# A decode attention and feed-forward kernel: products written over the keys, the output weights in two loads at the end, queries spread by two matmuls, quotients turned per 16 heads

## The chip, the cores and the metric

The kernel runs on one core of one Trainium2 chip. The metric is the device time of one execution in microseconds (us). A core has five engines that run side by side: TensorE (PE, matmuls and transposes; in a profile its weight loads stand apart as PEld), VectorE (DVE), ScalarE (ACT), GpSimd (POOL) and SyncE (SP), which here issues every transfer. Sixteen DMA engines move data between the HBM memory and SBUF, the core's working memory of 128 partitions; matmuls write to PSUM.

## The reference

One new token for each of four batch rows, model width 512, 32 heads of 128, 4096 cached keys and values per head, everything float32. The output mixes an attention block and a gated feed-forward block by a gate computed from the input:

```python
q = (x @ wq).reshape(B, Sq, H, Dh).transpose(0, 2, 1, 3)
scores = einsum("bhqd,bhkd->bhqk", q, k_cache) * (Dh ** -0.5)
p = softmax(scores, axis=-1)
o = einsum("bhqk,bhkd->bhqd", p, v_cache)
a = o.transpose(0, 2, 1, 3).reshape(B, Sq, H * Dh) @ wo
b = (gelu(x @ w_gate) * (x @ w_up)) @ w_down
g = sigmoid((x * gate_w).sum(-1, keepdims=True))
out = g * a + (1 - g) * b
```

With B = 4, H = 32, 4096 keys and Dh = 128, each cache has 268 MB. The weights wq and wo have 8.4 MB each, w_gate, w_up and w_down 3.7 MB each.

## The kernel before, in words

**Tiles.** The caches are cut into 64 tiles of keys and 64 of values. Tile i holds two heads (HT = 2) of one batch row: group g = i // 4, row b = i % 4. Each head has 64 partitions, and a partition holds 64 keys (or values) of 128 numbers, 32 KB in one piece. A tile has 4 MiB.

**Buffers and transfers.** A pool `kv` of five buffers of 32 KB a partition (NB = 5) takes every large load: wq in two halves, keys, values, the two feed-forward inputs (behind the values of 19 and 20) and w_down. The list `loads` (L79) fixes their order; `load_next` (L88) allocates a buffer for the next entry and issues its transfer on SP's queue. SP runs in program order, so a load that waits for its buffer holds back all loads behind it. A values load takes the buffer of a key tile, a keys load that of a values tile. wo comes apart from the list, in eight loads of 1 MB into a buffer of its own (`load_wo`, L95), each waiting for the matmuls that used the one before. w_down comes in four pieces, as the last transfer.

**Queries.** `po` holds x @ wq; eight PE transposes and eight copies make `QT` (L160 to L168). `q_spread` (L175) brings the queries of a group to all partitions of their head: eight matmuls of 128 columns, with a column of `QT` as broadcast weights.

**Scores.** There is one query per head and row, so scores are made on VectorE: `products` (L191) multiplies a part of the key tile by the query, `sums` (L203) adds up each 128. A tile is done in four parts (`MOST`, L34): four keys of the 64 whose sums ScalarE takes ("A", L209), and three times 20 with a VectorE sum ("D", L206). Products go to buffers of their own (`pa`, `pr`). The last two tiles give ScalarE more (`LAST`).

**Softmax.** `max_a` (L223) takes the maximum per partition and transposes it on PE; `soft_max` (L229) takes the maximum per head, spreads it by matmuls (L235), and lets ScalarE write the exponentials into `PM` and their sums into `RS` (L240). `pv` (L253) multiplies them by the values in 16 matmuls of 512 columns; a float32 matmul is two records in the trace, so 32 records.

**Output.** After the four rows of a group, `gather` (L265) copies the accumulated values and adds them up by matmuls, `weigh` (L275) divides by the sums of exponentials and turns the quotients by eight small matmuls (L286) into `oT`; after every second group `project_a` (L289) multiplies them by a quarter-megabyte slice of wo per step (L251) into `a_acc`. The feed-forward part runs inside tiles 20 and 21 (`ffn_up`, `ffn_gelu`) and `ffn_down` at the end.

**Order.** The program is written out by hand: each engine runs its instructions in the order in which the loop (L335) emits them. In iteration i VectorE makes the scores of tile i with the softmax of i-1 between its first parts, while PE does the values of i-1 and, behind them, the transpose of the maximum of i. In the last two iterations this order is changed so that maxima come earlier (L345 to L353).

Of the kernel before, what the change touches and what calls it, by code (L numbers as in the profile page):

```python
# [17 lines left out]
def tile_gated_mix(ctx: ExitStack, tc: tile.TileContext, x, kc, vc, wq, wo, w_gate, w_up, w_down, gate_w, out):  # L18
    nc = tc.nc
    P = 128  # L20
# [12 lines left out]

    MOST = (("A", 60, 64), ("D", 0, 20), ("D", 20, 40), ("D", 40, 60))  # L34
    LAST = (("U", 48, 56), ("A", 60, 64), ("D", 0, 20), ("U", 40, 48), ("A", 56, 60), ("D", 20, 40))
    NL = 2
    FFN_AT = 20
    FG = 512
# [9 lines left out]
    dump = head.tile([P, D], F32)  # L48
# [11 lines left out]
    def load(kind, i):  # L60
        t = T[kind, i] = kv.tile([P, TW], F32, name="kv")
        if kind in "kv":
            h, b = HT * (i // B), i % B
            src = (kc if kind == "k" else vc)[b, h:h + HT].rearrange("h (p r) d -> (h p) (r d)", p=PH)
            n = 2 if (kind, i) == ("v", NT - 1) else 1
            for s in range(n):
                nc.sync.dma_start(t[:, s * TW // n:(s + 1) * TW // n], src[:, s * TW // n:(s + 1) * TW // n])  # L67
        elif kind == "q":
            nc.sync.dma_start(t, wq.rearrange("(p c) n -> p (c n)", c=KC)[:, i * TW:(i + 1) * TW])
        elif kind == "f":  # L70
            nc.sync.dma_start(t[:, :KC * F], (w_gate, w_up)[i].rearrange("(p c) n -> p (c n)", c=KC))
        else:
            for f0 in range(0, F, FG):
                f1 = min(f0 + FG, F)
                n = (f1 - f0) // P
                nc.sync.dma_start(t[:, f0 // P * DM:(f0 // P + n) * DM],
                                  w_down[f0:f1].rearrange("(p i) n -> p (i n)", i=n))

    loads = [("q", 0), ("q", 1), ("k", 0)]  # L79
    for i in range(NT):  # L80
# [11 lines left out]

    WO = {}

    def load_wo(w):  # L95
        WO[w] = work.tile([P, 4, DM], F32, name="wo_sb", bufs=1)
        nc.sync.dma_start(WO[w], wo[w * 4 * D:(w + 1) * 4 * D, :].rearrange("(p e) n -> p e n", e=4))
# [52 lines left out]
    q_sb = work.tile([P, HG, D], F32, name="wo_sb", bufs=1)  # L150
    for c in range(KC):
        w = T["q", c // 2].rearrange("p (c n) -> p c n", c=2)[:, c % 2, :]
        for s in range(2):
            for j in range(4):
                n0 = (j * HG + s * HB) * D
                nc.tensor.matmul(PO[s][32 * j:32 * j + 32].rearrange("p j d -> p (j d)"), xT[:, c, :32],
                                 w[:, n0:n0 + HB * D], start=c == 0, stop=c == KC - 1)
    for s in range(2):
        nc.scalar.activation(q_sb[:, s * HB:(s + 1) * HB, :], PO[s], AF.Copy)
    QT = consts.tile([P, 4, HG, B], F32)  # L160
    for s in range(2):
        ps = ps1.tile([P, HB, P], F32, name="q")
        for a in range(HB):
            nc.tensor.transpose(ps[:, a, :], q_sb[:, s * HB + a, :], ident)
        for a in range(HB):
            nc.vector.tensor_copy(QT[:, :, s * HB + a, :],  # L166
                                  ps[:, a, :].rearrange("p (j b k) -> p j b k", j=4, b=B)[:, :, :, 0])
    QT = QT.rearrange("p j a b -> p (j a) b")  # L168
# [17 lines left out]
    u = consts.tile([P, 2, FG], F32)  # L186

    def parts(i):
        return LAST if i >= NT - NL else MOST

    def products(i, o):  # L191
        kind, r0, r1 = o
        g, b = divmod(i, B)
        n = r1 - r0
        if kind == "U":
            t = u.rearrange("p s (r d) -> p (s r) d", d=D)
        else:
            t = work.tile([P, n, D], F32, name="pa" if kind == "A" else "pr", bufs=1)
        nc.vector.tensor_tensor(t, T["k", i].rearrange("p (r d) -> p r d", d=D)[:, r0:r1],  # L199
                                QB[g][:, b:b + 1, :].to_broadcast([P, n, D]), op=OP.mult)  # L200
        return t

    def sums(i, o, t):  # L203
        kind, r0, r1 = o
        if kind == "D":
            nc.vector.tensor_reduce(SC[i][:, r0:r1], t, axis=AX.X, op=OP.add)  # L206
        else:
            for r in range(r0, r1):
                nc.scalar.activation(dump, t[:, r - r0, :], AF.Copy, accum_out=SC[i][:, r:r + 1])  # L209

    def scores_a(i):
        SC[i] = work.tile([P, R], F32, name="sc")
        return products(i, parts(i)[0])

    def scores(i, first):
        sums(i, parts(i)[0], first)
        for o in parts(i)[1:]:
            sums(i, o, products(i, o))
# [10 lines left out]
    def soft_max(i):  # L229
# [3 lines left out]
        nbp = ps2.tile([P, 1], F32, name="sm")  # L233
        for h in range(HT):
            nc.tensor.matmul(nbp[h * PH:(h + 1) * PH, :], ones[:1, :PH], m2[:, h:h + 1], start=True, stop=True)  # L235
        nb = work.tile([P, 1], F32, name="nb")
        nc.scalar.activation(nb, nbp, AF.Copy, scale=-scale)  # L237
        for h in range(HT):
            s = slice(h * PH, (h + 1) * PH)
            nc.scalar.activation(PM[i % 2][:, PZ:].rearrange("p (c m) -> p c m", m=32)[s, :, h:RJ * HT:HT],  # L240
                                 SC[i][s, :].rearrange("p (c j) -> p c j", j=RJ), AF.Exp, bias=nb[s, :], scale=scale,
# [32 lines left out]

    def weigh(g):  # L275
        ri = work.tile([B * HT, 1], F32, name="ri")
        nc.vector.reciprocal(ri, OS[g][:, D:])
        on = work.tile([B * HT, 4, D // 4], F32, name="on")
        nc.vector.tensor_scalar(on, OS[g][:, :D].rearrange("p (k e) -> p e k", e=4), ri, None, op0=OP.mult)  # L279
        w, r = divmod(g, 2)  # L280
        if r == 0:
            OT[w] = ps1.tile([P, 4, 32], F32, name="oT")
        for h in range(HT):
            q = 32 * (HT * r + h)
            for e in range(4):
                nc.tensor.matmul(OT[w][q:q + 32, e, :], on[:, e, :], hsel[:, h].rearrange("p b k -> p (b k)"),  # L286
                                 start=True, stop=True)

    def project_a(w):  # L289
        ot = work.tile([P, 4, 32], F32, name="ot")  # L290
        nc.scalar.activation(ot, OT[w], AF.Copy)
        for e in range(4):
            project(a_acc, ot[:, e, :], WO[w][:, e, :], (w, e) == (0, 0), (w, e) == (H // 4 - 1, 3))


    hT = consts.tile([P, F // P, 32], F32)

    def ffn_up(s):
        ps = ps1.tile([P, FG], F32, name="q")
        rest = F % FG  # L300
        nc.vector.memset(ps[32 * (F // FG):, rest:], 0.0)
        for c in range(KC):
            for j in range(4):
                n = min(FG, F - j * FG)
                nc.tensor.matmul(ps[32 * j:32 * j + 32, :n], xT[:, c, :32],
                                 T["f", s][:, c * F + j * FG:c * F + j * FG + n], start=c == 0, stop=c == KC - 1)
        nc.scalar.activation(u[:, s], ps, AF.Copy)

    def ffn_gelu():
        x1 = u[:, 0]  # L310
        s = T["f", 1].rearrange("p (a n) -> p a n", n=FG)
        t1, t2, t3, th, y, v = (s[:, a, :] for a in range(6))
# [5 lines left out]
        nc.vector.scalar_tensor_tensor(v, y, 0.5, u[:, 1], op0=OP.mult, op1=OP.mult)  # L318
        for j0, j1 in ((0, F // FG), (F // FG, 4)):
            w = min(FG, F - j0 * FG)  # L320
            n = w // P
# [89 lines left out]
```

## Time and profile before

| | before |
|---|---|
| median of 3 runs (lowest, highest) | 1318.66 us (1318.5, 1318.79) |
| the profiled execution, its own time | 1318.34 us |
| its span in the profile | 1316.6 us |
| VectorE busy | 1157.2 us (88%) |
| PE busy, PEld busy | 495.5 us (38%), 176.0 us (13%) |
| ScalarE busy | 210.5 us (16%) |
| moved by the DMA engines | 565.28 MB, 429 GB/s over the span |
| keys load: issue to landing, median | 42.3 us |
| values load: issue to landing, median | 33.5 us |

The span is what the profiler saw between the first and the last instruction; the profiled execution's own time is 1.74 us longer. In a row of a group, "x190 | 535.8, 2820 | 6.5" means 190 instructions, 535.8 us in sum, 2820 ns each on average, and 6.5 us of idle time just before them, with what ended it. In the chain and the timeline the first number is the start and the second the duration, both in us. The row of DMA digits gives the busy share of the 16 engines in tenths, in 40 equal slices. Queue q1 carries the kernel's transfers; q8 and q14 carry the engines' instructions.

### The profile page before, as it was taken

The page shows a single profiled execution, that of the slowest core. Times are in us where ns is not written, and L with a number is a line of the kernel's source. Part 1 is how long each engine was busy: PE and PEld are TensorE (multiplying, and loading weights), DVE is VectorE, ACT ScalarE, POOL GpSimd, SP SyncE. Part 2 cuts the span into 40 slices and gives each one's busy share as a digit, 9 for nine tenths or more (in the row PEclk, how much of TensorE's full clock was granted, in tenths as well). Part 3 has the DMA queues.
Part 4 walks back from the last instruction along what each step waited for, and adds up shares of the span by engine and source line. Part 5 has one row for each costly group of instructions (what it writes and reads, how often), then busy time and mean ns, then how long its engine had stood idle before and what let it go on. Part 6 is the DMA issues. An engine that isn't in the chain of part 4 may idle for free.

```text
span 1316.6 us, 9351 instructions
## 1 busy us (share of the span) xinstructions
PE 495.5 (38%) x3562; PEld 176.0 (13%) x3562; DVE 1157.2 (88%) x645; ACT 210.5 (16%) x963; POOL 0.7 (0%) x6
## 2 busy tenths in 40 slices
PE   3242434342441452433344243342433333343327
PEld 1011112110110110201112011110101111011102
DVE  1999899989999579998999989899899989999894
ACT  0111111101111111101101101101101101111133
POOL 0000000000000000000000000000000000000000
PEclk9566666666666676766666665776766765676667
DMA  9999999999999999999999999999999999999997
GB/s 411 433 429 430 432 433 437 433 430 431 431 436 434 428 435 432 432 433 437 430 432 432 433 438 431 433 432 431 433 434 432 433 433 430 436 434 430 434 430 331
DMA packets 21096, 565.28 MB, mean 429 GB/s; under 512 B 2472, under 2 KB 2488, under 8 KB 2620
## 3 DMA queue, kind: packets, MB, share of 16 engines
q1 hardware_dynamic: 21052, 564.69, 99.5%
q8 instruction: 28, 0.46, 0.1%
q14 instruction: 16, 0.13, 0.0%
HBM read 564.67 MB, written 0.01 MB: 429 GB/s over the span
## 4 chain that ended last, share of the span: by engine, by line
DMA 67%; DVE 29%; PE 2%; issue 1%; another core or an unknown queue 0%; SPq 0%; ACT 0%; DVEq 0%; ACTq 0%
DMA kv<-in_A_k_cache 54%; DVE pr L199 15%; DVE sc L206 12%; DMA kv<-in_A_v_cache 10%; DMA kv<-in_B_w_down 2%; PE po L258 2%; DVE pa L199 1%; DVE m L232 0%; SPq L67 0%; PE b_acc L251 0%; DVE u L199 0%; DVE on L279 0%; PE sm L138 0%; DVE m L225 0%
## 5 line engine op out<-in xcount | busy, mean ns | idle before, releaser
L258 PE MATMUL po<-kv,pm 128*32 128x512 f32 x2048 | 365.1, 877 | 489.0 <-DMA kv<-in_A_v_cache 486.4
L206 DVE TENSOR_REDUCE sc<-pr 128x20 f32<-128x2560 f32 x190 | 535.8, 2820 | 6.5
L199 DVE TENSOR_TENSOR pr<-kv,qb 128x2560 f32<-128x2560 f32 x190 | 535.3, 2817 | 4.2
L258 PEld LDWEIGHTS po<-kv,pm 128*32 128x32 f32 x2048 | 91.1, 154 | 707.4 <-issue 692.1
L199 DVE TENSOR_TENSOR pa<-kv,qb 128x512 f32<-128x512 f32 x66 | 45.5, 690 | 85.8 <-DMA kv<-in_A_k_cache 85.8
L237 ACT ACTIVATE nb<-sm 128x1 f32<-128x1 f32 x64 | 10.9, 170 | 573.4 <-PE sm L235 573.2
L227 PE MATMUL sm<-ident,m 128*1 128x128 f32 x64 | 19.2, 300 | 206.1 <-DVE m L225 205.9
L209 ACT ACTIVATE dump<-pa 128x128 f32<-128x128 f32 x264 | 81.7, 309 | 10.4 <-DVE pa L199 2.6
L235 PE MATMUL sm<-m,ones 1*64 1x1 f32 x256 | 22.3, 238 | 85.9 <-DVE m L232 85.9
L182 ACT ACTIVATE qb<-q 128x512 f32<-128x512 f32 x16 | 9.6, 597 | 258.6 <-PE q L179 258.6
L209 ACT ACTIVATION_READ_ACCUMULATOR dump<-pa 128x1 f32 x264 | 49.2, 186 | 0.0
L240 ACT ACTIVATE pm<-sc,nb 64x64 f32<-64x64 f32 x128 | 44.5, 348 | 3.0 <-ACT nb L237 0.2
L267 ACT ACTIVATE o<-po 128x512 f32<-128x512 f32 x16 | 9.6, 597 | 191.2 <-PE po L258 191.2
L227 PEld LDWEIGHTS sm<-ident,m 128*1 128x1 f32 x64 | 5.1, 79 | 250.7 <-issue 219.3
L235 PEld LDWEIGHTS sm<-m,ones 1*64 1x64 f32 x256 | 17.0, 181 | 103.8 <-DVE m L232 96.3
L179 PE MATMUL q<-ident,QT 128*64 128x128 f32 x256 | 24.9, 357 | 0.6 <-DVE QT L166 0.6
L240 ACT ACTIVATION_READ_ACCUMULATOR pm<-sc,nb 64x1 f32 x128 | 23.6, 185 | 0.0
L270 PE MATMUL sm<-o,sel 128*8 128x128 f32 x128 | 16.6, 273 | 10.7 <-ACT o L267 10.7
L179 PEld LDWEIGHTS q<-ident,QT 128*64 128x64 f32 x256 | 19.7, 181 | 4.3 <-issue 2.7
L225 DVE TENSOR_REDUCE m<-sc 128x1 f32<-128x64 f32 x64 | 14.1, 220 | 6.6
L232 DVE TENSOR_REDUCE m<-sm 1x2 f32<-1x128 f32 x64 | 17.4, 272 | 1.1 <-PE sm L227 1.1
L270 PEld LDWEIGHTS sm<-o,sel 128*8 128x8 f32 x128 | 10.3, 89 | 26.7 <-ACT o L267 24.9
(56 smaller groups left out, 132.3 us busy)
## 6 DMA issues: line engine op xcount, KB each, us to landing
kv<-in_A_k_cache SPq DMA_DIRECT2D x64, 4096.0 KB, 42.3
kv<-in_A_v_cache SPq DMA_DIRECT2D x63, 4096.0 KB, 33.5
kv<-in_A_wq SPq DMA_DIRECT2D x2, 4096.0 KB, 16.4
wo_sb<-in_A_wo SPq DMA_DIRECT2D x8, 1024.0 KB, 39.9
kv<-in_A_v_cache SPq DMA_DIRECT2D x2, 2048.0 KB, 39.6
kv<-in_B_w_gate SPq DMA_DIRECT2D x1, 3584.0 KB, 43.1
kv<-in_B_w_up SPq DMA_DIRECT2D x1, 3584.0 KB
kv<-in_B_w_down SPq DMA_DIRECT2D x3, 1024.0 KB, 30.1
```

What stands on the lines that cost most here:

```text
L179: nc.tensor.matmul(ps[h * PH:(h + 1) * PH, b, :], QT[:, HT * g + h, b:b + 1].to_broadcast([P, PH]), ident, start=True, stop=True)
L199: nc.vector.tensor_tensor(t, T["k", i].rearrange("p (r d) -> p r d", d=D)[:, r0:r1], QB[g][:, b:b + 1, :].to_broadcast([P, n, D]), op=OP.mult)
L206: nc.vector.tensor_reduce(SC[i][:, r0:r1], t, axis=AX.X, op=OP.add)
L209: nc.scalar.activation(dump, t[:, r - r0, :], AF.Copy, accum_out=SC[i][:, r:r + 1])
L225: nc.vector.tensor_reduce(m1, SC[i], axis=AX.X, op=OP.max)
L227: nc.tensor.transpose(MT[i], m1, ident)
L232: nc.vector.tensor_reduce(m2, MT[i].rearrange("o (h p) -> o h p", h=HT), axis=AX.X, op=OP.max)
L235: nc.tensor.matmul(nbp[h * PH:(h + 1) * PH, :], ones[:1, :PH], m2[:, h:h + 1], start=True, stop=True)
L237: nc.scalar.activation(nb, nbp, AF.Copy, scale=-scale)
L240: nc.scalar.activation(PM[i % 2][:, PZ:].rearrange("p (c m) -> p c m", m=32)[s, :, h:RJ * HT:HT], SC[i][s, :].rearrange("p (c j) -> p c j" ...
L258: nc.tensor.matmul(PO[g % 2][32 * c:32 * c + 32].rearrange("p j d -> p (j d)"), PM[i % 2][:, m0:m0 + 32], T["v", i][:, j * N:(j + 1) * N], ...
L270: nc.tensor.matmul(OS[g][:, :D], sel[:, j].rearrange("p b h -> p (b h)"), o[:, j, :], start=j == 0, stop=j == RJ - 1)
```

## The change

It does the following, part by part:

- **Scores.** A product is written over the keys it was made from, in two halves; one sum over the whole tile follows. ScalarE takes no sums any more, and the buffers `pa`, `pr` and `dump` are gone. The last two tiles are done as all others.
- **Softmax.** The negative maxima of both heads come from one matmul with two columns.
- **Queries.** `po` is masked and folded to a [128, 128] tile `qd` (partition: four head blocks, row and head), and `QM` holds it once per row, masked. `q_spread` is one matmul of 512 columns per head with a mask as broadcast weights.
- **Quotients.** They are collected in `ONA` for eight groups (16 heads) and turned by 32 matmuls at once (`turn`, `turned`), twice in the whole run instead of eight small matmuls per group.
- **wo.** It comes in two loads into the `kv` buffers. The first half stands behind the keys of tile 63, before the values of 61; the second is the last transfer of all, in three pieces. A row in SBUF is one piece of memory; a partition's row lies 16 rows of wo (32 KB) behind or 256 rows (512 KB) apart from its neighbour's.
- **w_down.** One load of whole rows of 28 KB, in front of the second half of wo.
- **Feed-forward.** Width is split into four times 448 instead of 512 and a rest; the activations are turned by 14 VectorE transposes of 32x32 blocks instead of PE transposes and copies.
- **End.** `project_a(0)` runs in iteration 62; after the loop come the softmax and values of 63, w_down's matmuls in three parts with gather, weigh and turn between them, and wo's second half last.

```diff
@@ loads @@
+        elif kind == "d":
+            nc.sync.dma_start(t[:, :FC * DM], w_down.rearrange("(p i) n -> p (i n)", i=FC))
         else:
-            for f0 in range(0, F, FG):
...
+            src = wo[i * HW * D:(i + 1) * HW * D].rearrange("(g s e) n -> s g (e n)", s=HT * D // E, e=E)
+            ends = WO_END if i else (0, E)
+            for e0, e1 in zip(ends, ends[1:]):
+                nc.sync.dma_start(t[:, e0 * DM:e1 * DM], src[:, :, e0 * DM:e1 * DM])
...
-        loads += [("k", j) for j in ((i + 1,) if i + 1 < NT - NL else (NT - 2, NT - 1) if i == NT - NL - 1 else ())]
-        loads.append(("v", i))
+        loads += [("k", i + 1), ("v", i)]
...
-    loads.append(("d", 0))
+    loads[-1:] = [("k", NT - 1), ("w", 0)] + [("v", i) for i in range(NT - 3, NT)] + [("d", 0), ("w", 1)]
@@ queries @@
+    for s in range(2):
+        nc.vector.tensor_tensor(u[:, s].rearrange("p (a d) -> p a d", d=D), PO[s],
+                                amask[:, s * HB:(s + 1) * HB, None].to_broadcast([P, HB, D]), op=OP.mult)
+    nc.vector.tensor_reduce(qd, u.rearrange("p s (a d) -> p d (s a)", d=D), axis=AX.X, op=OP.add)
+    nc.vector.tensor_tensor(QM, qd[:, None, :].to_broadcast([P, B, D]), bmask[:, :, None].to_broadcast([P, B, D]),
+                            op=OP.mult)
...
-        for b in range(B):
-            for h in range(HT):
-                nc.tensor.matmul(ps[h * PH:(h + 1) * PH, b, :], QT[:, HT * g + h, b:b + 1].to_broadcast([P, PH]),
-                                 ident, start=True, stop=True)
+        for h in range(HT):
+            j, a = divmod(HT * g + h, HG)
+            nc.tensor.matmul(ps[h * PH:(h + 1) * PH].rearrange("p b d -> p (b d)"),
+                             hmask[:, j, a:a + 1].to_broadcast([P, PH]), QM.rearrange("p b d -> p (b d)"),
+                             start=True, stop=True)
@@ scores @@
+    def products(i, r0, r1):
         g, b = divmod(i, B)
+        t = T["k", i].rearrange("p (r d) -> p r d", d=D)[:, r0:r1]
+        nc.vector.tensor_tensor(t, t, QB[g][:, b:b + 1, :].to_broadcast([P, r1 - r0, D]), op=OP.mult)
+
+    def sums(i):
         SC[i] = work.tile([P, R], F32, name="sc")
+        nc.vector.tensor_reduce(SC[i], T["k", i].rearrange("p (r d) -> p r d", d=D), axis=AX.X, op=OP.add)
@@ quotients @@
+        nc.vector.tensor_scalar(ONA[:, :, :, g % (HW // HT)], OS[g][:, :D].rearrange("p (k e) -> p e k", e=E), ri, None,
+                                op0=OP.mult)
+    def turn(w):
+        OT[w] = ps1.tile([P, E, 32], F32, name="oT")
         for h in range(HT):
+            for e in range(E):
+                nc.tensor.matmul(OT[w][h * PH:(h + 1) * PH, e, :], ONA[:, e].rearrange("p k g -> p (k g)"),
+                                 hsel[:, h].rearrange("p b k -> p (b k)"), start=True, stop=True)
@@ feed-forward @@
+        for i in range(FC):
+            nc.vector.transpose(hT[:, i, :], v[:, i::FC])
@@ the loop and the end @@
+        products(i, 0, RA)
+        if i > 0:
             soft_max(i - 1)
         if pair:
             weigh(g - 1)
+        products(i, RA, R)
+        sums(i)
         load_next()
+        if i > 0:
             pv(i - 1)
             load_next()
...
+        max_a(i)
...
+        if i == NT - 2:
+            project_a(0)
+            load_next()
+    soft_max(NT - 1)
     pv(NT - 1)
-    ffn_down(0)
+    ffn_down(0, 5)
     gather(H // HT - 1)
+    ffn_down(5, 9)
     weigh(H // HT - 1)
+    turn(H // HW - 1)
+    turned(H // HW - 1)
+    ffn_down(9, FC)
+    tb = consts.tile([P, C4], F32)
+    nc.vector.tensor_scalar(tb, b_acc, g_cols[:, 1:2], None, op0=OP.mult)
+    project_a(H // HW - 1)
     res = work.tile([P, C4], F32, name="res")
+    nc.vector.scalar_tensor_tensor(res, a_acc, g_cols[:, 0:1], tb, op0=OP.mult, op1=OP.add)
```

More of the change, by code (lines that the diff above doesn't have):

```diff
@@ L47, in tile_gated_mix @@
     hsel = head.tile([B * HT, HT, B, 8], F32)
-    dump = head.tile([P, D], F32)
+    qd = head.tile([P, D], F32)
     xT = head.tile([P, KC, 4, B, 8], F32)
@@ L232, in soft_max @@
         nc.vector.tensor_reduce(m2, MT[i].rearrange("o (h p) -> o h p", h=HT), axis=AX.X, op=OP.max)
[L233 to L236, printed above, removed]
+        nbp = ps2.tile([P, HT], F32, name="sm")
+        nc.tensor.matmul(nbp, ones[:1, :], m2, start=True, stop=True)
+        nb = work.tile([P, HT], F32, name="nb")
         nc.scalar.activation(nb, nbp, AF.Copy, scale=-scale)
@@ L298, in ffn_up, with turned, project_a @@
+    OTS = {}
+    def turned(w):
+        OTS[w] = work.tile([P, E, 32], F32, name="ot", bufs=1)
+        nc.scalar.activation(OTS[w], OT[w], AF.Copy)
+    def project_a(w, e0=0, e1=E):
+        for e in range(e0, e1):
+            project(a_acc, OTS[w][:, e, :], T["w", w][:, e * DM:(e + 1) * DM], (w, e) == (0, 0),
+                    (w, e) == (H // HW - 1, E - 1))
+    hT = consts.tile([P, FC, 32], F32)
     def ffn_up(s):
         ps = ps1.tile([P, FG], F32, name="q")
-        rest = F % FG
```

144 lines of the change are left out of this document (32 added, 112 removed).

## The prediction

> **What bounds the kernel now.** I read the page's busy and DMA rows first, then the sync engine's own waits, one middle stretch of the timeline, and the chain at the end.
>
> ```profile
> span 1316.6 us, 9351 instructions
> ...
> PE 495.5 (38%) x3562; PEld 176.0 (13%) x3562; DVE 1157.2 (88%) x645; ACT 210.5 (16%) x963; POOL 0.7 (0%) x6
> ...
> DMA  9999999999999999999999999999999999999997
> ...
> q1 hardware_dynamic: 21052, 564.69, 99.5%
> q8 instruction: 28, 0.46, 0.1%
> q14 instruction: 16, 0.13, 0.0%
> ```
>
> Nothing is as full as the 16 DMA engines: 564.69 MB keep them at 99.5% of the span, and no slice but the last is below 9 tenths. A tile of 4 MiB takes 9.7 us (4.19 MB at 432 GB/s), a head pair (keys and values) 19.35 us. VectorE (DVE) has 18.1 us of work in that time. So only three things can move the time: a queue that runs dry, packets that take longer or shorter, and what stands behind the last byte.
>
> ```profile
> SPq L67 <- DVE pr L199: 912.9, 61, 17.8
> ```
>
> This is the sync engine's wait table: it mostly waits for the last product of a key tile, since that frees the buffer for the next values. What this costs is seen in a middle stretch of the timeline:
>
> ```profile
> 706.68 0.33 SPq L67 DMA_DIRECT2D kv<-in_A_v_cache  x1
> 706.69 2.82 DVE L206 TENSOR_REDUCE sc<-pr 128x20 f32<-128x2560 f32 x1
> 707.54 0.33 SPq L67 DMA_DIRECT2D kv<-in_A_k_cache  x1
> ...
> 729.82 0.69 DVE L199 TENSOR_TENSOR pa<-kv,qb 128x512 f32<-128x512 f32 x1 [1.10 <-DMA kv<-in_A_k_cache]
> ```
>
> The keys awaited at 729.82 are those queued just before 706.68. So the values load issued at 706.68 stands behind 23 us of transfers. Over the whole trace the least such margin is 16.2 us (issue at 83.38); behind the feed-forward part it is 19.6 us (issue at 493.13).
>
> The end, from the chain, and the DMA share in 40 slices of 1300 to 1317:
>
> ```profile
> 1277.72 31.11 DMA kv<-in_B_w_down
> 1308.88 1.08 PE b_acc L251 x32
> 1309.96 0.53 PE oT L286 x16
> 1310.85 1.08 PE a_acc L251 x32
> 1311.93 1.35 PE b_acc L251 x48
> 1313.31 0.35 DVE res L387
> ```
> ```profile
> DMA  9999899999999986865656656422000000000000
> ```
>
> TensorE (PE) finishes at 1313.28; 3.3 us follow (res, the store, its landing). The DMA share falls in steps from 1306 on: in the trace's packet records six engines write their last byte at 1306.1 to 1308.0, ten at 1310.6 to 1312.2. All have the same data; the difference is instruction fetches (q8, q14). A q8 fetch takes 0.93 us, and the 32 KB packet beside it 1.70 instead of 1.213: 1.43 us lost. The 28 go round eight engines, so some have three (4.3 us late) and three have four (5.7). The stream ends with the latest engine, at 1312.2.
>
> **The change, part by part.** The sum is made against the profiled execution, 1318.34 us (span 1316.6 and 1.74 around it); the median shown is 1318.66, 0.3 above, so I add 0.3 at the end.
>
> ```profile
> L206 DVE TENSOR_REDUCE sc<-pr 128x20 f32<-128x2560 f32 x190 | 535.8, 2820 | 6.5
> L199 DVE TENSOR_TENSOR pr<-kv,qb 128x2560 f32<-128x2560 f32 x190 | 535.3, 2817 | 4.2
> ...
> L199 DVE TENSOR_TENSOR pa<-kv,qb 128x512 f32<-128x512 f32 x66 | 45.5, 690 | 85.8 <-DMA kv<-in_A_k_cache 85.8
> ```
>
> *Scores.* The product rows give (2817-690)/2048 = 1.04 ns an element and 0.16 us fixed: a half tile of 4096 elements costs 4.41 us, two 8.82. The sum rows (2820 for 2560, 220 for L225's 64) give 1.042: 8.69 us for 8192. Together 17.5 us a tile against 0.69+3x5.64 = 17.6 before: VectorE no longer leaves four rows of 64 to ScalarE, but has three fixed costs in place of seven. With maxima and gaps it stays at 18.0 of 19.35 us. No row shows a product that overwrites its operand. [...] ScalarE loses the 296 L209 pairs (147 of its 210.5 us; it is on no path but the exponentials'). The products also wait for an older load into the same buffer, long landed: 0.
>
> *Release of the keys.* It moves behind the sum: 14.9 us after the start before (32.20 to 47.09 for the first tile), now 17.5. Values loads are issued 2.7 us later, behind 20 us of queue instead of 23, and 13 at the tightest. Cost 0. If that cover were gone, each us of lateness would cost a us per tile. The keys loads stand behind them on SP and move with them; POOL's queue issues nothing here.
>
> *Feed-forward.* Six PE transposes and four copies become 14 VectorE transposes, 128x32. Not in the trace: between L166's 128x16 copy (167 ns) and L225 (220), 2.3 to 3.1 us, against 0 at least. The keys behind them start later and values follow 2.7+2.8 late on the 19.6 us margin: cost 0, cover 14 us.
>
> *Queries, maxima, turns.* Query spread: 8 matmuls of 128 columns become 2 of 512 per pair; L235 2 to 1; L286 128 to two times 32. At the head, two masked products (0.7 each), a strided sum of 1024 (about 1.2), QM (0.7), two wide matmuls (1.5) and a copy (0.6) run from 26.2 to about 32, where the first keys land (32.2). Even 3 us late costs nothing: the queue is 23 us deep then (issue at 47.09). The maximum of tile i-1 is now read behind 4.4 us of product instead of 0.6; exponentials then end 6.6 us after the keys start, values land at 9.7.
>
> *The loads.* Bytes are equal. By the packet records 32 KB takes 1213 ns, 28 KB 1062, 8 KB 309, 4 KB 159 (20 KB interpolated 761). wo: 1024 of 8 KB (316 engine-us) become 128 each of 32, 20, 8, 4 KB (313); w_down 139 becomes 136. That is 7 engine-us, -0.43 us on 16 engines. Eight wo loads leave the middle, with SP's 28.5 us of waits for a_acc; they come behind the keys of 63 (first half) and as the very last (second half).
>
> *Instruction fetches.* [...] 24 fetches leave three per engine at most: -1.43 us; 0 if one engine still gets four. [...] The stream ends at 1312.2-0.43-1.43 = 1310.3; call it X.
>
> *The tail.* Behind the values of 61 come 9.7+9.7+8.5+9.8 = 37.7 us of transfers. VectorE's product of 63 starts early, but the maximum of 62 between its halves needs PE's transpose, which stands behind the probabilities times values of 61. So from X-37.7: semaphore 0.4, those 32 matmuls 6.0 (rows 5.1 to 6.5), transpose and maximum 0.8, second half 4.4, sum 8.7 (PE meanwhile does the first wo, 128 records in 4.4 to 7.7 us, and the block of 62, and is done about as early), maximum to exponentials 2.6 (as 1280.28 to 1282.9), 32 matmuls of 63 6.0, then at L251's 34 ns a record: 40 records of w_down 1.35, gather 0.9, 32 records 1.1, turn 64 records 2.2 (16 take 0.53), 40 records 1.35, wo 128 records at 28 to 34 ns 4.0. Sum 39.8: PE ends at X+2.1 = 1312.4. The floor, when only the last piece counts, is the 1.05 us of before: X+1.05 = 1311.4. Against 1313.28 that is -0.9; range -1.9 to +1.5 (6.5 for each block, fetches unchanged). The last loads are in time: w_down waits for the matmuls of 61, 13 us before its turn, the last wo for the first wo's use, about 14.
>
> The two blocks of 32 start at clock 0.50, as the windows 1280 to 1290 show, with 1.00 only from 1305. [...] The trace has blocks of 5.1, but most are longer, and I keep 6.0.
>
> **The rivals.**
>
> A. *The transfers end it* (the tail's PE chain is shorter): X+1.05, -1.9: 1316.7. For: the pairs at full clock. Against: the wait above.
>
> B. *The fetches do not shrink on the latest engine*: everything 1.4 later than forecast, +0.5: 1319.1.
>
> C. *The wo loads read slowly.* Their rows for one engine lie 512 KB apart, the caches' 32 KB. No row has such a stride; the trace's slowest packets, the first sixteen, took 1.6 to 2.0 us instead of 1.213. At 1.82, sixteen rows' worth an engine cost +9.7, straight on the bound: 1327; from 1.43 us a packet (+3.5) it decides. Against: 16403 of the 16512 packets of 32 KB take 1213 ns, wq's among them, whose rows lie 64 KB apart. [...]
>
> D. *VectorE becomes the bound* through products in place. It decides from 1.35 us a tile, 15% on the products; at 20% it is (18.0+1.76-19.35)x62 = +25: 1343. For: 18.0 of 19.35 us are full. Against: no row slower per element.
>
> E. *The tail at half clock or with one more wait*: the 10.9 us behind the last values grow by up to 9: +2 to +8, 1320 to 1326; from +3.5 it decides. For: PE idles some 4 us before them. Against: clock 1.00 behind 1305 now.
>
> **How the numbers follow.** Forecast 0.45, A 0.18, B 0.13, C 0.06, D 0.05, E 0.13. Forecast: 1318.34-0.9+0.3 = 1317.7; I say 1317.6. Of the first three, 0.06 falls under 1316.0. 0.2% (2.6 us) is about what a measurement can tell from no change: faster 0.06, same 0.72 (with a part of E), slower 0.22. The range goes from A's lower edge, 1316.0, into E, 1321.5; C and D stay out.
>
> **What would show it.** Right: q8 with 24 fetches or so, all engines' last data by 1310.5, products at 4.4 and sums at 8.7 us, VectorE idle some 13 us inside tile 63, values loads still 20 us ahead. Wrong: products over 5 us (D); wo packets of 32 KB over 1.3 us (C); slices under 9 in the middle (a dry queue); matmuls of 60 ns in the last 10 us (E).

## The result, and the profile after

The changed kernel takes 1341.01 us (median of 6 runs, 1340.58 to 1343.62), the kernel before 1318.51 (6 runs, 1318.36 to 1318.79): a ratio of 1.0174, with a 95% interval of 1.0161 to 1.0187. It is 22.5 us slower. The forecast was 1317.6, the range ended at 1321.5.

First the page of the changed kernel: span, busy time by engine, the busy share of the 16 DMA engines and what they moved in 40 slices of 33.5 us, and the DMA queues.

```profile
span 1339.0 us, 7575 instructions
...
PE 506.5 (38%) x3100; PEld 174.4 (13%) x3100; DVE 1162.4 (87%) x399; ACT 90.3 (7%) x359; POOL 0.7 (0%) x6
...
DMA  9999999999999999999999999999999999999997
GB/s 407 438 423 438 435 426 437 433 429 437 432 430 437 428 435 435 427 436 434 429 436 432 430 436 433 429 438 432 430 436 430 433 434 432 432 436 431 290 396 210
...
q1 hardware_dynamic: 20044, 564.69, 99.5%
q8 instruction: 24, 0.39, 0.1%
```

The GB/s row of the page before, for comparison:

```profile
GB/s 411 433 429 430 432 433 437 433 430 431 431 436 434 428 435 432 432 433 437 430 432 432 433 438 431 433 432 431 433 434 432 433 433 430 436 434 430 434 430 331
```

The busy share of the DMA engines is that of before: 99.5% again, for the same 564.69 MB. The row to read is GB/s. Behind the first slice, 36 slices stand at 423 to 438, as before (428 to 438). Then it drops to 290 and, in the last slice, to 210 (430 and 331 before), while the row above shows 9 and 7 in these places in both kernels. The engines are busy and move half as much: longer packets, not a dry queue.

The same in windows of 10 us (length, then busy time of TensorE, its weight loads, VectorE, ScalarE and GpSimd with instruction counts, then TensorE's clock, DMA share, GB/s):

```profile
1240.00:1250.00 10.00, 2.08 (x12) 0.58 (x3) 9.10 (x5) 0.41 (x2) 0.00 (x0) 0.67 1.07 429
1250.00:1260.00 10.00, 0.00 (x0) 0.00 (x0) 9.90 (x2) 0.63 (x4) 0.00 (x0) 0.50 0.99 213
1260.00:1270.00 10.00, 0.00 (x0) 0.00 (x0) 6.55 (x3) 0.00 (x0) 0.00 (x0) 0.50 1.01 220
...
1310.00:1320.00 10.00, 5.39 (x48) 1.71 (x44) 0.00 (x0) 0.60 (x1) 0.00 (x0) 0.84 1.04 236
1320.00:1330.00 10.00, 10.00 (x166) 9.00 (x160) 0.60 (x2) 0.60 (x1) 0.00 (x0) 0.67 0.88 214
```

Half the rate, in just the stretches in which the two halves of wo are on their way. In the packet records a 32 KB packet takes 2.4 us there, where one of keys takes 1.213 (170 took over 2.2 us: by number and time, wo's 128 and some of the keys and values beside them); the mean for 20 KB is 1.42 (forecast 0.761), for 8 KB 0.48 (0.309), for 4 KB 0.23 (0.159). Behind the first 60 us all packets together took 379 engine-us more than at the sizes' usual durations, 23.7 us on 16 engines, against 1.2 us in the kernel before. Those 22.5 us more, less the 0.4 that the larger pieces save, are 22.1.

The chain of after ends in the transfers too (start, length, what):

```profile
1293.27 3.63 PE a_acc L228 x128
...
1297.56 0.59 SPq L80
...
1298.20 36.81 DMA kv<-in_A_wo
1335.02 0.04 issue
1335.06 0.69 PE a_acc L228 x16
1335.75 0.02 issue
1335.77 0.35 DVE res L358
```

Before, TensorE ended at 1313.28 behind a last byte at 1312.20; now the last byte comes at 1334.08 (21.9 later, the 22.1 just worked out), 16 records follow, and it ends at 1335.75 (22.5 later). Nothing else is behind the data.

The middle of the run is as forecast. The groups of the scores (count, then busy us, mean ns of one, idle before):

```profile
L192 DVE TENSOR_TENSOR kv<-kv,qb 128x4096 f32<-128x4096 f32 x128 | 564.9, 4414 | 78.4 <-DMA kv<-in_A_k_cache 76.6 <-ACT qb L184 1.8
L196 DVE TENSOR_REDUCE sc<-kv 128x64 f32<-128x8192 f32 x64 | 555.9, 8686 | 6.3
```

and the sync engine's waits (total us, times, longest), which answer to the line of before with 912.9 us:

```profile
SPq L68 <- DVE m L203: 1108.7, 62, 19.4
```

A product in place takes 4.414 us and a sum 8.686 (forecast 4.41 and 8.69). On this row the sync engine waits 196 us more, because the keys' buffer is freed later; its other waits shrank (for the landing of keys from 156.6 us to 43.4), and no slice shows a dry queue: the wait moved into the cover that the prediction named.

### The profile page after: what moved, and what is told of

Same layout as the page of the kernel before. It is cut to its first block, busy times and chain, and to the rows that moved or that the text cites. A ratio compares the mean times of both kernels' runs of the same rounds, so it can differ in the third digit from the quotient of the medians.

```text
span 1339.0 us, 7575 instructions
## 1 busy us (share of the span) xinstructions
PE 506.5 (38%) x3100; PEld 174.4 (13%) x3100; DVE 1162.4 (87%) x399; ACT 90.3 (7%) x359; POOL 0.7 (0%) x6
## 3 DMA queue, kind: packets, MB, share of 16 engines
q1 hardware_dynamic: 20044, 564.69, 99.5%
## 4 chain that ended last, share of the span: by engine, by line
DMA 60%; DVE 37%; PE 2%; issue 1%; ACT 0%; SPq 0%; DVEq 0%; ACTq 0%
DMA kv<-in_A_k_cache 53%; DVE kv L192 18%; DVE sc L196 18%; DMA kv<-in_A_v_cache 3%; DMA kv<-in_A_wo 3%; DMA kv<-in_A_wq 2%; PE po L235 0%; DVE m L203 0%; PE po L151 0%; DVE m L210 0%; PE q L286 0%; PE a_acc L228 0%; DVE ONA L257 0%; PE sm L205 0%; PE q L180 0%
## 5 line engine op out<-in xcount | busy, mean ns | idle before, releaser
L192 DVE TENSOR_TENSOR kv<-kv,qb 128x4096 f32<-128x4096 f32 x128 | 564.9, 4414 | 78.4 <-DMA kv<-in_A_k_cache 76.6
L196 DVE TENSOR_REDUCE sc<-kv 128x64 f32<-128x8192 f32 x64 | 555.9, 8686 | 6.3
L212 PE MATMUL sm<-m,ones 1*128 1x2 f32 x128 | 37.0, 356 | 319.7 <-DVE m L210 319.7
L212 PEld LDWEIGHTS sm<-m,ones 1*128 1x128 f32 x128 | 31.5, 304 | 351.0 <-DVE m L210 343.7
L214 ACT ACTIVATE nb<-sm 128x2 f32<-128x2 f32 x64 | 11.0, 172 | 815.3 <-PE sm L212 815.3
L180 PE MATMUL q<-QM,hmask 128*64 128x512 f32 x64 | 24.3, 848 | 3.4 <-DVE QM L168 3.4
L151 PE MATMUL po<-kv,xT 128*32 128x512 f32 x64 | 10.9, 846 | 3.1 <-DMA kv<-in_A_wq 2.7
L265 PE MATMUL oT<-hsel,ONA 8*64 8x32 f32 x128 | 10.6, 257 | 0.0
```

The lines of the kernel that those rows point to most:

```text
L180: nc.tensor.matmul(ps[h * PH:(h + 1) * PH].rearrange("p b d -> p (b d)"), hmask[:, j, a:a + 1].to_broadcast([P, PH]), QM.rearrange("p b d ...
L192: nc.vector.tensor_tensor(t, t, QB[g][:, b:b + 1, :].to_broadcast([P, r1 - r0, D]), op=OP.mult)
L196: nc.vector.tensor_reduce(SC[i], T["k", i].rearrange("p (r d) -> p r d", d=D), axis=AX.X, op=OP.add)
L212: nc.tensor.matmul(nbp, ones[:1, :], m2, start=True, stop=True)
```

## The experiments

Three theories for the doubled packets were set against each other. A: memory. The rows that a transfer reads one after the other lie 512 KB apart. B: the order of the partitions. The load's outermost dimension is 16 long; the supposition is that each DMA engine then gets eight neighbouring partitions, and that two engines at a time write the same group of partitions. C: a load pattern of three dimensions is slow by itself.

**wo read in order.** The pattern of this load alone is undone, all else stays. The projection then multiplies the quotients with other rows of wo.

```diff
-            src = wo[...].rearrange("(g s e) n -> s g (e n)", s=HT * D // E, e=E)
+            src = wo[...].rearrange("(p e) n -> p (e n)", e=E)
...
-                nc.sync.dma_start(t[:, e0 * DM:e1 * DM], src[:, :, e0 * DM:e1 * DM])
+                nc.sync.dma_start(t[:, e0 * DM:e1 * DM], src[:, e0 * DM:e1 * DM])
```

> The changed kernel with one edit: the two halves of wo are read row by row, partition p getting the p-th 32 KB of the half (a plain pattern of 128 rows) instead of 16 times 8. The rows then meet the wrong quotients, so the attention part of the output is another; the bytes, the packets, the order and all engines' work stay. All three theories of the slow wo loads (A: their rows lie 512 KB apart in memory; B: the first dimension of 16 gives each DMA engine eight neighbouring partitions, and pairs of engines write to the same group of partitions; C: a pattern of three dimensions is slow by itself) expect packets of 1213, 761, 309 and 159 ns again and the 22 us gone: about 1318, and by the terms of the prediction 1317.6 (1316.7 where the transfers end it). If the time stays near 1341, wo is not the cause.

Measured: 1319.8 us (10 runs, 1317.68 to 1321.32) against 1318.53 (13 runs), a ratio of 1.0007 (0.9997 to 1.0017). Windows of this kernel in the stretch where the first half of wo moves:

```profile
1250.00:1260.00 10.00, 0.00 (x0) 0.00 (x0) 9.90 (x2) 0.83 (x4) 0.00 (x0) 0.50 1.01 436
1260.00:1270.00 10.00, 0.00 (x0) 0.00 (x0) 6.75 (x3) 0.00 (x0) 0.00 (x0) 0.50 0.99 429
```

436 and 429 GB/s in place of 213 and 220. wo's packets usually take 1213, 761, 309 and 159 ns, the forecast's durations, and the last data come at 1310.74 (forecast 1310.3). The whole loss sits in the pattern of this load. What is left of the change costs nothing that can be told from zero.

**Near rows in the slow pattern, far rows in the plain one.** Two kernels load keys in wo's place (the projection multiplies these instead), the first with 16 times 8 rows that lie close together in memory, the second with 128 plain rows 512 KB apart (shown together; the second also takes `src[:, e0 * DM:e1 * DM]`).

```diff
+            rows = kc.rearrange("b h (r q) d -> (b h r) (q d)", q=R)
-            src = wo[...].rearrange("(g s e) n -> s g (e n)", ...)
+            src = rows[i * 144:(i + 1) * 144].rearrange("(s g) n -> s g n", g=9)[:, :8]   # near
+            src = rows[:2048].rearrange("(p m) n -> p m n", m=16)[:, i]                   # far
```

> The changed kernel with wo's loads replaced by equally large ones from the key cache, in the same pattern of 16 times 8 rows into the same partitions, but with rows that lie close: eight neighbouring rows of 32 KB per outer step, one row skipped. wo itself is not read, so the attention part of the output is wrong. A (distance in memory): as fast as rows in order, 1317 to 1319, packets of 1213 ns. B (partitions per engine) and C (three dimensions): as slow as the changed kernel, 1341, packets of about 2.4 us.

> The changed kernel with wo's loads replaced by equally large ones from the key cache in a plain pattern of 128 rows that lie 512 KB apart. wo itself is not read, so the attention part of the output is wrong. A: slow, 1341 or above, since all 128 rows now have that distance. B and C: fast, 1317 to 1319, packets of 1213 ns.

Near in the slow pattern: 1341.58 us. Far in the plain pattern: 1317.76 us (one run each, before 1318.53). The window of 1250 to 1260, near first:

```profile
1250.00:1260.00 10.00, 0.00 (x0) 0.00 (x0) 9.90 (x2) 0.61 (x4) 0.00 (x0) 0.50 0.99 213
```
```profile
1250.00:1260.00 10.00, 0.00 (x0) 0.00 (x0) 9.90 (x2) 0.72 (x4) 0.00 (x0) 0.50 1.00 433
```

Theory A falls on both sides: near rows are slow (213 GB/s), and the packets of rows 512 KB apart take 1213 ns (433 GB/s).

**Plain rows in two halves.** wo in order again, each load cut into partitions 0 to 63 and 64 to 127; every pattern has two dimensions. The edit is against the kernel of the first experiment.

```diff
-                nc.sync.dma_start(t[:, e0 * DM:e1 * DM], src[:, e0 * DM:e1 * DM])
+                for p0 in (0, PH):
+                    nc.sync.dma_start(t[p0:p0 + PH, e0 * DM:e1 * DM], src[p0:p0 + PH, e0 * DM:e1 * DM])
```

> The kernel with wo's rows in order, each load cut into two of 64 partitions (0 to 63, then 64 to 127), plain two-dimensional patterns of neighbouring rows. The attention part of the output is another, as there. B: sixteen engines write to half of the partitions at a time, so pairs share again and the loads take twice as long: about 1340. A and C: 1318, with at most 1 us for four more transfers.

Measured: 1343.39 us (one run), 20 KB packets 1452 ns (median), and in the same window:

```profile
1250.00:1260.00 10.00, 0.00 (x0) 0.00 (x0) 9.90 (x2) 0.68 (x4) 0.00 (x0) 0.50 1.02 216
```

Theory C falls as the one cause: a plain two-dimensional load is as slow when it covers 64 partitions (216 GB/s). That three dimensions cost something beside it is not excluded, but B foretold all four runs, and with 213 and 216 GB/s it leaves nothing over. So here it is the set and order of the partitions that decides: 213 and 216 GB/s for the two shapes, against 429 to 436 for 128 plain partitions. That engines in pairs write to the same partitions, and share one way into SBUF there, was the author's estimate; no run shows it, since a packet record doesn't name its engine or its partition.

**The pattern in the kernel before.** If B holds, the old kernel must lose by it too. Its eight wo loads of 1 MB get the 16 by 8 pattern (the projection again meets other rows).

```diff
-        nc.sync.dma_start(WO[w], wo[w * 4 * D:(w + 1) * 4 * D, :].rearrange("(p e) n -> p e n", e=4))
+        nc.sync.dma_start(WO[w].rearrange("p e n -> p (e n)"),
+                          wo[w * 4 * D:(w + 1) * 4 * D, :].rearrange("(g s e) n -> s g (e n)", s=16, e=4))
```

> The kernel before with one edit: each of its eight loads of wo in the pattern of 16 times 8 rows (8 KB each, 128 KB apart) over the same partitions. The rows meet the wrong quotients, so the attention part of the output is another. B (pairs of engines write to the same partitions): each load takes 4.9 us instead of 2.4, in the middle of the stream, and nothing hides it: +19.5 us, 1338, with the packets of these loads near 620 ns. Rival (only large packets or the end of the run suffer): below 1322.

Measured: 1358.16 us (one run, before 1318.43): +39.7 and not +19.5. The GB/s row of the page, with a dent for each of the eight loads:

```profile
GB/s 404 433 434 397 432 433 432 387 433 434 432 431 392 437 432 433 432 372 432 432 432 432 372 433 430 433 432 369 432 433 432 432 356 432 433 432 396 387 432 290
```

The direction holds, the size is double. The 8 KB packets of wo take 561 ns on average instead of 309, 16.1 us on 16 engines. More than that comes from their neighbours: 32 KB packets of keys and values beside them take up to 2.9 us, and all packets of this size together 20.6 us more on 16 engines than in the kernel before. Together 36.7 of the 39.7. The other 3.0 are time in which an engine had no packet: up to the last byte 4.2 us for each engine on average, against 1.2 before. The neighbours are plain loads. That engines leave a slow load at different times and then meet on the same partitions is the author's explanation; no run isolates it. In the changed kernel the same is seen at the edges, where 34 of w_down's 128 packets of 28 KB, next to wo's second half, took 1.92 us on average instead of 1.062.

**wo in order, with quotients to fit.** The quotients are laid out so that wo's natural rows serve: they are masked per head, and one matmul of 128 columns of weights does both heads of a step, 32 records in place of 64.

```diff
-    ONA = consts.tile([B * HT, E, D // E, HW // HT], F32)
+    ONA = consts.tile([B * HT, E, HW // HT, HT, D // E], F32)
...
-        for h in range(HT):
-            for e in range(E):
-                nc.tensor.matmul(OT[w][h * PH:(h + 1) * PH, e, :], ONA[:, e].rearrange("p k g -> p (k g)"),
-                                 hsel[:, h].rearrange("p b k -> p (b k)"), start=True, stop=True)
+        for e in range(E):
+            nc.tensor.matmul(OT[w][:, e, :], ONA[:, e].rearrange("p g h k -> p (g h k)"),
+                             hb.rearrange("p b k -> p (b k)"), start=True, stop=True)
```

> The changed kernel with wo's rows in order and the quotients turned to fit: each group's quotients are written twice, masked by head, so that one matmul per step gives all 128 rows in wo's own order (16 matmuls in place of 32). All loads are plain patterns over 128 partitions. If the pairing of engines on partitions is the whole loss, this is the rest of the change: the transfers end at 1310.7 as with rows in order, and PE behind them has 32 records fewer to turn than there. Theory: PE's chain still ends the kernel, 1.5 to 2 us earlier than with rows in order, 1316.5 to 1319, with the same spread of some 3 us by the clock of the last 15 us. Rival (the transfers already end it): 1316.9 with a spread under 1 us.

Measured: 1321.31 us (11 runs, 1317.93 to 1321.98), ratio 1.0014 (1.0005 to 1.0023): slower than expected. The last data came at 1310.6, so the tail is what misses. Its turn and what follows, from the timeline (start, length):

```profile
1304.55 4.35 PE L269 MATMUL oT<-hb,ONA 8*128 8x32 f32 x32
...
1308.83 2.36 PE L228 MATMUL b_acc<-kv,hT 128*32 128x128 f32 x40
...
1310.97 5.33 PE L228 MATMUL a_acc<-kv,ot 128*32 128x128 f32 x128
```

Half the records make the turn no shorter: 4.35 us, where 64 records of half the width took 3.84 in the first experiment. So it goes by the columns of its weights: at full clock a record of 128 takes 118 ns (3.78 us for 32 in the run with fillers in the gap, below) and one of 64 takes 58 (3.71 us for 64 in the run with far rows). Here the last 1.4 us of the turn are at half clock. Behind it, w_down's 40 records take 2.36 us, not 1.35: TensorE's clock stands at 0.50 from 1307.53 to 1314.36.

**The maximum of 62 earlier.** If VectorE's wait in tile 63 sets the end, taking `max_a(62)` ahead of `pv(61)` must bring the time to the last transfer.

```diff
+            if i == NT - 2:
+                max_a(i)
             pv(i - 1)
...
-        max_a(i)
+        if i != NT - 2:
+            max_a(i)
```

> The kernel with wo's rows in order and quotients to fit, and in iteration 62 the transpose of the maximum of 62 in front of the matmuls of 61 instead of behind them. Theory: the 12.9 us in which VectorE waits for that transpose inside tile 63 set PE's end; without them the matmuls of 63 end near 1298, PE waits for the last transfers and ends 1.05 us behind them, at 1311.8: 1318.34 - (1313.28 - 1311.8) = 1316.9 for the execution, spread under 1 us, faster than before by 0.1%. Rival (the order of these steps does not matter, the clock in the turn does): as the kernel without the move, with its spread.

Measured: 1322.95 us (6 runs), ratio 1.0026 (1.0014 to 1.0037). VectorE's wait inside tile 63 is gone and the values of 63 are done at 1294.55 (1301.57 in the kernel it was made from), and the time does not go down: that theory falls. From the timeline:

```profile
1301.10 2.36 PE L228 MATMUL b_acc<-kv,hT 128*32 128x128 f32 x40 [6.54 <-DMA kv<-in_B_w_down]
```

TensorE now idles 6.54 us until w_down is there, and its clock stands at 0.50 from 1298.99 to 1305.82 and, from within the turn on, from 1309.23 to 1316.06. The end is set by work and clock in the tail.

**More instruction fetches.** To price these, 488 matmuls of one column are added to the tiles 1 to 61 of that kernel.

```diff
+            if i < NT - 2:
+                for _ in range(8):
+                    nc.tensor.matmul(b_acc[:32, :1], xT[:, 0, :32], ones[:, :1], start=True, stop=True)
```

> The kernel with the early maximum and, in tiles 1 to 61, eight idle matmuls of one column each (488 in all, 1952 PE instructions more, written to a sum that is begun anew later). Theory of the fetches: 7 or 8 more q8 packets, one more for each of eight DMA engines, the last engine done 1.4 us later, and so the kernel 1.4 us slower than without them (1318.3 if that one takes 1316.9). Rival: instruction fetches cost nothing at the end, the time stays within 0.3 us of it. PE's own time cannot matter there: it is 38% busy and the idle matmuls take about 0.5 us a tile.

Measured: 31 fetches, against 24 in the kernel it was made from:

```profile
q8 instruction: 31, 0.51, 0.1%
```

The last data come at 1312.33 instead of 1310.47: 1.86 us later, expected 1.4. The kernel's time, 1323.2 (4 runs), is only 0.3 above the one it was made from, which is what the rival expected: its end hangs on TensorE, so the later data hide. The fetches' price is shown on the stream, not on the time.

**Turn ahead of w_down.** The thin turn is put into the 6.5 us in which TensorE idled.

```diff
     pv(NT - 1)
-    ffn_down(0, 5)
     gather(H // HT - 1)
-    ffn_down(5, 9)
     weigh(H // HT - 1)
     turn(H // HW - 1)
     turned(H // HW - 1)
-    ffn_down(9, FC)
+    ffn_down(0, FC)
```

> The kernel with wo read in order and the maximum of tile 62 taken early, with the last four steps in another order: gather, weigh, turn and the copy stand ahead of all of w_down's matmuls instead of in between. The thin turn (32 records of 32 columns, 4.4 us) then falls into the 6.5 us in which TensorE waited for w_down (1294.55 to 1301.1), and behind it there is only dense work of 34 ns a record. Theory 'the clock in the tail sets the end' (a thin turn late in the tail halves the clock of what follows): turn ends about 1302.5, 112 records of w_down at half clock end about 1309, the clock is back before wo's 128 records, which end 1311 to 1313; 3.3 us more to the end of the span as in the kernel it is made from, so a span of 1314.5 to 1316.5 and a median of 1316 to 1318, below the kernel before (1318.5). Rival 'the amount of work behind the last load sets it': TensorE has the same records in both orders and only 6.5 us of idle to fill, of which the turn takes 4.4: 1322.9 - 4.4 = 1318.5, level with the kernel before. Rival 'the clock stays at half whatever the order': wo's records end at 1316 to 1317, a median of 1321.

Measured: 1317.64 us (11 runs, 1316.53 to 1319.89) against 1318.44 (15 runs), ratio 0.9993 (0.9984 to 1.0002). From the timeline:

```profile
1297.32 5.99 PE L269 MATMUL oT<-hb,ONA 8*128 8x32 f32 x32 [1.00 <-DVE ONA L262]
...
1303.24 5.92 PE L228 MATMUL b_acc<-kv,hT 128*32 128x128 f32 x112
...
1308.98 3.67 PE L228 MATMUL a_acc<-kv,ot 128*32 128x128 f32 x128
```

5.3 us less than the kernel it came from. Most of this, 4.4 us, is the turn moved into idle time, which the rival of the amount of work had too (1318.5). The clock's part shows in the records: half clock lasts from 1298.50 to 1308.74 and ends ahead of wo's 128 records, which take 3.67 us instead of 5.21. It is the fastest of the versions that give the reference's output. Its interval still holds 1.

**Filler matmuls in the gap.** With the tail's first order, 12 matmuls of 512 columns, unread, behind the last values.

```diff
     pv(NT - 1)
+    warm = ps1.tile([P, B, D], F32, name="q")
+    for _ in range(12):
+        nc.tensor.matmul(warm.rearrange("p b d -> p (b d)"), ident, QM.rearrange("p b d -> p (b d)"), start=True, stop=True)
     ffn_down(0, 5)
```

> The kernel with wo read in order and the maximum of tile 62 taken early, order of the tail unchanged, with 12 matmuls of 512 columns whose result nobody reads put behind the last values, where TensorE waited 6.54 us for w_down and the clock fell to 0.50 at 1298.99. Theory 'idle TensorE lowers the clock': the clock is 1.00 when w_down comes, its 40 records take 1.35 us instead of 2.36 and the gather 0.9 instead of 1.91: 2.0 us less ahead of the turn; if the turn (4.4 us of thin records) then still halves the clock of what follows, the median is 1321.0; if the clock stays full through the turn, 40 records 1.35 for 2.36 and wo's 128 records 4.0 for 5.2 as well: 1318.7. Rival 'the clock in the tail is set from elsewhere': no change, 1322.9.

Measured: 1323.5 us (5 runs, 1323.38 to 1325.75), expected 1318.7 to 1321. The fillers took 0.88 us each, 10.57 in all for a gap of 6.54, so they ended 4 us behind w_down's arrival:

```profile
1294.62 10.57 PE L356 MATMUL q<-QM,ident 128*128 128x512 f32 x24
...
1305.12 1.30 PE L228 MATMUL b_acc<-kv,hT 128*32 128x128 f32 x40
...
1308.30 3.78 PE L269 MATMUL oT<-hb,ONA 8*128 8x32 f32 x32
...
1312.01 2.36 PE L228 MATMUL b_acc<-kv,hT 128*32 128x128 f32 x40
```

As a kernel it loses; as a measurement it is clean. With TensorE kept dense the clock stays 1.00 through the gap, the 40 records take 1.30 us for 2.36, and the turn 3.78 for 4.46. Right behind the turn, the next 40 records of w_down take 2.36 again. So it is the turn that halves the clock here, with hardly any idle time on TensorE: it is busy for 1.90 of the 2.00 us from 1308 and 2.00 of the 2.00 from 1310, at a clock of 1.00 and 0.98, and the clock is 0.50 in the 2.00 us from 1312.

**Fillers inside the turn.** Four fillers go into the version with the turn ahead: one before the gather, one behind it, two between the turn's records.

```diff
+            if between and e % 6 == 5:
+                between()
             nc.tensor.matmul(OT[w][:, e, :], ...
```

> The kernel with gather, weigh and turn ahead of w_down (1317.64 us), with four matmuls of 512 columns whose result nobody reads: one ahead of the gather, one behind it, two inside the turn (0.88 us each, as the twelve of the kernel with filler matmuls took). Theory 'TensorE's clock follows how dense its last microseconds were': the clock stays 1.00 through the turn, which takes 3.8 us and 1.8 for the two fillers and ends about 1303 as before, but w_down's 112 records then take 3.7 us instead of 5.9 and end about 1306.8, ahead of wo's last transfer (1310.5); its last 16 records end about 1311.2 instead of 1312.65: 1.4 us less, a median of 1316.2. Rival 'the turn alone lowers the clock, whatever lies between its records': w_down again takes 5.9 us, 1317.6 or up to 1 us more for the fillers. Rival 'the last transfer is not what is left': the end moves by the full 2.2 us of w_down, 1315.4.

Measured: 1318.04 us (11 runs, 1317.07 to 1322.28), ratio 1.0000 (0.9991 to 1.0009): a miss, by 1.8 us, and the time of the first rival. The second filler of the turn and w_down, from the timeline:

```profile
1301.93 2.03 PE L359 MATMUL q<-QM,ident 128*128 128x512 f32 x2
...
1306.16 4.54 PE L228 MATMUL b_acc<-kv,hT 128*32 128x128 f32 x112
```

The clock fell at 1302.01 all the same, just as the second filler began. In the 3.4 us before, one filler of 1.1 us among 2.3 us of the turn's records did not hold it, and the fillers cost their own time.

## Why the prediction was wrong, point by point

- **The loads (the step that failed).** "The loads" took wo's packets at the sizes' usual durations (1213, 761, 309, 159 ns) and got -0.43 us. They took nearly twice as long; with the neighbours' losses that is 22.5 us on the full queue. The step priced a packet by its size alone. The run with wo read in order gives each of those four durations as the usual one, so the prices were right for 128 plain partitions, and it was the pattern of the partitions, in the diff for all to see, that was not looked at.
- **Rival C** named the place and the sign (wo's loads, straight on the bound, deciding from 1.43 us a packet) with a chance of 0.06. Its cause, memory rows 512 KB apart, is refuted by two runs, and its price of +9.7 came from the slowest packets that the trace had, 1.82 us; 2.4 were met. Its sign, packets over 1.3 us, came, with another cause. The packets of other strides, wq's 64 KB among them, were taken as the reason for a small chance; none of them had 16 by 8 partitions.
- **Scores, release of the keys, feed-forward, queries.** Right, and seen at 1.0007 without the load: 4.414 and 8.686 us (that a product in place neither gains nor loses was an assumption until this run); no slice under 9 in the middle; the 14 transposes took 0.191 us each, 2.7 together (2.3 to 3.1 forecast). D did not occur.
- **Instruction fetches.** 24, as forecast, though no run shows how many instructions one fetch brings; what the runs show is 28 fetches before, 24 after, and 31 against 24 with 488 matmuls more; the stream, without the load's loss, ended at 1310.74 (1310.3). Added fetches delayed it by 1.86 us. B did not occur.
- **The tail.** In the changed kernel it hardly counts, since the transfers end it. In the run with wo read in order VectorE waited 12.85 us in tile 63 (13 forecast) and TensorE ended at 1315.44 (1312.4). Two terms were mis-sized: the turn, 3.77 us for 2.2, because 64 records were priced from 16 narrower ones (8x32 weights against 8x64), and w_down's 40 records behind it, 2.29 for 1.35, at half clock. That is much like rival E, but the cause is not TensorE's idling ahead of the values; it is the turn (the clock is 1.00 from 1301.95 and falls within the turn, at 1308.78). Three of its ten runs, at 1317.7 to 1317.8, match the forecast of 1317.6, and so does the run with far rows, 1317.76. In part that is luck: there the turn takes 3.71 us for 2.2, the values of 63 take 5.13 for 6.0 and wo's 128 records 3.68 for 4.0. One reading of before was off as well: its clock is back at 1.00 from 1300.76, not only from 1305.

## What to carry to other kernels

Price a load by the partitions that it covers and their order, not by its bytes and rows alone: a load of 64 partitions (216 GB/s), or one split as 16 times 8 (213), halved the rate of a full queue here (429 to 436), and slowed the plain loads beside it as well (34 packets of w_down took 1.92 us instead of 1.062). GB/s by slice showed this loss at once (290 and 210 in the changed kernel), where the busy share showed nothing (9 and 7 tenths, as before). Where the time is set by a full queue, a reordering that suits the compute (rows in the order in which the quotients are turned) is cheap only if it leaves the transfer's partitions alone (here it did not, and cost 22.5 us); do it on the compute side, as the version with the turn ahead does, whose time can't be told from that of before.

## What the runs showed of the hardware that was not expected

- Two shapes of load run at half the rate: 16 outermost groups of 8 partitions (213 GB/s, 2.4 us for 32 KB), and 64 partitions (216 GB/s). Rows 512 KB apart in memory cost nothing (433 GB/s).
- In the kernel before with the 16 by 8 pattern, the slow loads of 1 MB cost more in the neighbours (20.6 us over eight loads) than in themselves (16.1).
- TensorE's clock falls to half while TensorE is busy, if the work is thin, as here: in the run with fillers in the gap, behind a turn of 3.78 us with at most 0.1 us of idle time beside it. In the tails of all these profiles (the last 45 us before TensorE ends) the stretches between two changes of the clock last 3.413 us or a multiple of it (at half clock 1308.78 to 1312.19 with wo read in order; 1307.53 to 1314.36 with quotients to fit), and so they do in the whole profiles of the kernel before and the changed one (1 to 14 times 3.413), so each profile can be cut into windows of that length. In these two, at full clock, the windows were counted by the time in them that is idle, turn or the softmax's matmuls of one row. In the kernel before, 66 windows end in a fall, each with 2.03 us or more of such time, and 50 do not, each with 1.99 us or less; in the changed kernel 67 with 2.04 or more and 46 with 1.97 or less. In the tails of the other runs the turn alone does it: 3.41 us of it in the run with wo read in order, 2.15 in the run with more fetches, 2.28 beside one filler. From half clock it rose only behind windows with at most 0.76 us of such time in the kernel before, 0.82 in the changed one. The gather's records count as work: in the run with the maximum of 62 earlier, the window up to 1305.82, with 1.74 us of them and 1.68 of w_down's, ends in a rise.
- So it matters where a turn falls in these windows. In the run with far rows, they meet at 1306.16 and the turn is shared out, 1.93 us and 1.70 us; the clock stays 1.00 to the end, and w_down's 40 records behind it take 1.30 us:

```profile
1304.22 3.71 PE L266 MATMUL oT<-hsel,ONA 8*64 8x32 f32 x64
...
1307.86 1.30 PE L229 MATMUL b_acc<-kv,hT 128*32 128x128 f32 x40
```

  This fits the scatter of the run with wo read in order (1317.7 or 1319.4 to 1321.3).
